# Attention in 32 units with 32x64 score products, ahead of a gated FFN

## The chip, the cores and the metric

The kernel runs on one core of a Trainium2 chip. The metric is the device time of one execution in microseconds (us). Engines carry the names of the profile: PE (TensorE matmul; PEld is its weight load), DVE (VectorE), ACT (ScalarE), POOL (GpSimd), SP (SyncE, which issues the loads). L12 is line 12 of the kernel.

## The reference

```python
def _attn_ref(q, k, v):                       # q, k, v: (8, 8, 576, 64)
    scores = scale * np.matmul(q, k.transpose(0, 1, 3, 2))
    rel = pos[:, None] - pos[None, :]
    mask_local = (rel >= 0) & (rel < stride)          # stride 32, heads 0 to 3
    mask_strided = (rel >= 0) & (pos[None, :] % stride == pos[:, None] % stride)
    scores = np.where(masks[None], scores, -1e9)      # then a softmax over keys
    return np.matmul(attn, v)

def _moe_ref(x, w_gate, w_val, w_out, rms_g):   # x: 4608 tokens of 8 heads x 64 = 512
    rms = np.sqrt(np.mean(x * x, axis=-1, keepdims=True) + 1e-06)
    xn = x / rms * rms_g
    g = xn @ w_gate                                   # 512 -> 1536
    silu = g * (1.0 / (1.0 + np.exp(-g)))
    return silu * (xn @ w_val) @ w_out                # 1536 -> 512
```

A query of heads 0 to 3 sees the 32 latest keys; a query of heads 4 to 7 sees the keys at distance 0, 32, 64, ..., so after a sort of the sequence by position modulo 32 (the "residue order") its at most 18 keys are neighbours.

## The kernel before

**FFN.** Tokens come in nine chunks of 512. For chunks 0 to 6 a chunk runs through 12 slots `u` of 128 hidden columns. In a slot, `slot_g` and `slot_v` issue 12 matmuls each into the banks `g` and `v` (L971), ACT and DVE form silu(g) x v in the tile `e` (L984, L986, L997), `slot_h` splits it into a float32r high and low part (`hh` L1004, `hl` L1013), and `slot_o` of the slot before issues 12 matmuls (L1028) into the four `acc` banks. All of these are 128x128 by 128x512 float32r matmuls, three for each product of split operands; weights and activations are split into high and low parts on the chip. Each 12 matmuls into a bank end in work on ACT and DVE before that bank is free again. Chunks 7 and 8 are taken together by `pair_of_chunks`, with seven products of sums of blocks in place of eight (L1357, L1522); their operands (`raw`, sums of `raw` halves, high and low parts) are built beforehand on DVE, ACT and POOL.

**Attention.** It makes the `raw` chunks that the FFN reads; tokens of chunk c+1 are made while chunk c runs. There are 96 work units: a batch row, a pair of heads `p` and a third `j` of the sequence, each of up to two tiles of 96 queries (heads 0 to 3) or of 126 and 108 (heads 4 to 7) for both heads. For a unit, `step_s` issues the scores on PE, adds the mask, finds the row maxima (DVE), exponentiates each tile (ACT, L694, with the sum), and normalizes (POOL, L703); `step_t` transposes the probabilities; `step_o` multiplies by the values (L783) for groups of up to four units and copies the result to `raw` (L818 ACT, L820 DVE). Scores have three forms: the first units add the mask on PE (L644) and multiply float32 queries by keys that lie in weight slots with the other head's rows at zero (L650); a few then use plain float32 products of 64 rows (L654) with the mask on DVE; from unit 27 on, q and k are split into high and low parts (`split`: ACT L541, DVE L546) and a tile is one float32r matmul of 128x256 (L639), whose two halves DVE adds with the mask (L675, L679, L681) ahead of the maximum (L682). Transposes are PE products against an identity (L757, copied out at L761) for the first 21 units and 32x32 stream transposes on DVE (L746) later.

**From chunk to chunk.** When the `raw` tile of a chunk is complete, squares are added up in `ssq`, a product with ones (L876, two matmuls; L857 for chunk 1, L838 for chunk 0) gives the sum over the 512 features in every partition, ACT takes the root (L912), DVE the reciprocal in four parts (L915) and scales `raw` (L919), and `convert` splits it into `xh` and `xl` (L932, L947), which the first `g` matmuls of the chunk read. `last_root` does the same for chunk 8 (L1110, L1114, L1117, L1119).

**Order.** Work is recorded with a cost, what it reads and writes, and a due time; the class `Plan`, a list scheduler, then fixes the order of instructions on every engine. `CO = 99` leaves PE's order free; `BA` and `BM` shift the due times of attention and of the FFN. The prologue does the first 15 units, with weights being loaded and split on DVE, ACT and POOL through chunk 0.

Of the kernel before, what the change touches and what calls it, by code (L numbers as in the profile page):

```python
# [34 lines left out]
RES = [7, 7, 6, 6, 6]  # L35
RES0 = [0, 7, 14, 20, 26]
NEG = -1.0e9
NCST = 510
# [16 lines left out]
BA = 30000.0  # L55
BM = 60000.0
# [60 lines left out]
CO = 99  # L117
# [32 lines left out]
class Plan:  # L150
# [7 lines left out]
    def __init__(self):  # L158
        self.ops = []
        self.writer = {}  # L160
        self.readers = {}
        self.lengths = []
        self.serial = False
        self.last_pe = None
        self.early = []
        self.lift = []
        self.boost = 0.0

    def op(self, eng, cost, at, fn, reads=(), writes=(), bytes_=0, rel=0.0, lock=(), tab=None, port=False, chain=False, also=None, early=0.0):
# [16 lines left out]
        deps.discard(i)  # L186
        if eng == "PE":
            if self.serial:
                deps.add(self.last_pe)
            self.last_pe = i  # L190
# [40 lines left out]
    def latest(self, users, took, length):  # L231
# [7 lines left out]
        for _ in range(n):  # L239
# [12 lines left out]
            for d in ops[i][1]:  # L252
                t = start[i] + (0.0 if on[d] == e and not ops[d][2] else self.lat(i)) + long[d] - ops[d][0][on[d]][0] + self.early[d]
                ready[d] = max(ready[d], t)
# [5 lines left out]
    def forward(self, users, due, hold, due2=None, hold2=None):  # L260
# [6 lines left out]
        def enter(i):  # L267
            ways, deps, _, rel, _, _, _ = ops[i]
            ready[i] = {e: max([end[d] + (0.0 if on[d] == e and not ops[d][2] else self.lat(i)) for d in deps] + [rel]) for e in ways}
# [74 lines left out]
def attn_moe(ctx: ExitStack, tc: tile.TileContext, qT: bass.AP, kT: bass.AP, vl: bass.AP, vs: bass.AP,  # L344
# [12 lines left out]
    ident = sbt([P, P], "ident")  # L357
    cb = sbt([P, 382], "cb", BF16)
    mloc = cb[:LQ, 0:256].rearrange("p (t k) -> p t k", k=P)
    m7 = cb[:126, 256:382]  # L360
    m6 = cb[:108, 256:364]
# [16 lines left out]
    def pair_of(i):  # L378
        k = (i % NPAIRS if i < 12 else i % 2) if i < n_pro else 0
        if k:  # L380
            return (acc01, acc23)[k - 1] if k == 2 else acc01, k, (f"a{2 * k - 2}", f"a{2 * k - 1}")
        return pair_, 0, ("b0", "b1")
    banks = {"g": bank["g"], "v": bank["v"], "b0": pair_[:, 0], "b1": pair_[:, 1], "a0": acc[0], "a1": acc[1], "a2": acc[2], "a3": acc[3]}
    mxs = [sbt([P, 2, 2], f"mx{i}") for i in range(2)]
    raw = [sbt([P, KC, CH], f"raw{i}") for i in range(NX)]
    low = sbt([P, QKN], "qk")
    stat = [mxs + [sbt([P, 2, 2], f"mx{i}") for i in range(2, 4)], [sbt([P, 2, 2, 2], f"su{i}") for i in range(4)]]
    SW = S + PAD
    xx = [sbt([P, SW], f"xx{i}") for i in range(2)] + [low[:, SW * i:SW * i + SW] for i in range(3)]
    vts = [sbt([P, 2, NLT, D], f"vt{i}") for i in range(2)]  # L390
    spare = [sbt([P, CH], f"x{n}{kc}") for n in "hl" for kc in range(KC)]
    pbuf = [sbt([P, CH], f"pp{i}") for i in range(NPB)]
    rcol = few[:, 12:16]
    tbufs = [sbt([P, CH], f"pT{i}") for i in range(NTB)]
    tbuf = tbufs[0]
# [44 lines left out]
    for x in range(5):  # L440
        op("Pool", 100, -1, lambda x=x: nc.gpsimd.memset(xx[x][:, 0:PAD], 0.0), writes=[("xp", x)])
    for x in range(NPB):
        op("Pool", 600, -1, lambda x=x: nc.gpsimd.memset(pbuf[x], 0.0), writes=[("pp", x)])

    for i in range(4):
        op("Pool", 70, -1, lambda i=i: nc.gpsimd.memset(stat[1][i][:, :, :, 1:2], 1e-9), writes=[("st", i)])
# [1403 lines left out]
```

## Time and profile before

| what | value |
|---|---|
| runs | 1012.08, 1014.07, 1016.27 us (median 1014.07) |
| profiled execution, its span | 1011.5 us |
| first and last 128x512 matmul of the FFN | starts at 32.70 us, ends at 1007.42 us |
| granted PE clock | 0.9 and 0.7 of full speed in the first two slices of 25 us, then 0.9 or more |
| attention on PE, records of matmuls | L783 704, L639 252, L650 88, L654 114, L757 78, L644 30 |

The page gives, for each engine, the time it was busy as a share of the span, the chain of work that ended last, and groups of instructions by line. A float32 matmul leaves two records, a float32r or bfloat16 matmul one. Matmuls are pipelined, so a matmul's duration on the page (about 0.39 us for a 128x512 one) is longer than the distance from its start to the next start; that distance is what a matmul costs.

### The profile page before, as it was taken

Reading aid. Unit: us, or ns where it says so; the run is one execution under the profiler, and the core shown is the slowest. Engines: PE = TensorE matmul, PEld = TensorE weight load, DVE = VectorE, ACT = ScalarE, POOL = GpSimd, SP = SyncE. Lnnn points to the kernel's source line nnn. Section 1 sums busy time; section 2 is a strip of 40 time slices with the busy share of each in tenths; the row PEclk is TensorE's granted clock in tenths of the full one; section 3 lists DMA queues with packets and bytes.
Section 4 is the critical chain, followed back from the end, with each engine's and each line's share of the span. In section 5 each row is a group of like instructions: output and inputs, shape, how many; then the busy total and the mean of one; then the engine's idle time right before and its main releaser. Section 6 shows DMA issues by size and latency. Waiting matters only on the chain.

```text
span 1011.5 us, 15391 instructions
## 1 busy us (share of the span) xinstructions
PE 991.0 (98%) x5104; PEld 805.3 (80%) x5104; DVE 844.7 (84%) x1745; ACT 572.0 (57%) x1502; POOL 417.3 (41%) x390
## 2 busy tenths in 40 slices
PE   8899998999999999999999999999999999999998
PEld 6678775888878888878878888887888878888886
DVE  5699999898888788679888878788988798988891
ACT  7899867554755555455555565555555444344440
POOL 6222457324662332533425432256643343565300
PEclk9799999999999999999999999999999999999999
DMA  9886342532432331532242422333332101120452
GB/s 314 271 286 227 129 137 98 177 109 91 161 133 92 102 124 61 178 99 93 92 132 94 141 97 105 99 116 118 114 114 79 42 1 42 39 87 1 156 167 73
DMA packets 52559, 121.11 MB, mean 120 GB/s; under 512 B 5312, under 2 KB 21248, under 8 KB 52480
## 3 DMA queue, kind: packets, MB, share of 16 engines
q1 hardware_dynamic: 51712, 119.28, 35.3%
q10 hardware_dynamic: 768, 0.85, 0.3%
q8 instruction: 40, 0.66, 0.3%
q14 instruction: 39, 0.32, 0.1%
HBM read 98.09 MB, written 22.02 MB: 119 GB/s over the span
## 4 chain that ended last, share of the span: by engine, by line
PE 80%; DVE 12%; ACT 3%; DMA 2%; issue 2%; ACTq 0%; DVEq 0%
PE g L971 18%; PE v L971 18%; PE acc L1028 18%; PE g L1357 3%; PE v L1357 3%; PE pair L1357 3%; PE pair L783 3%; PE pair L639 3%; DVE qk L546 2%; PE v L1522 2%; PE acc L1522 2%; PE acc L1357 2%; PE g L1522 2%; DVE raw L919 1%; DVE pT L746 1%
## 5 line engine op out<-in xcount | busy, mean ns | idle before, releaser
L971 PE MATMUL g<-xh,wg 128*128 128x512 f32 x672 | 211.8, 397 | 4.4 <-DVE e L986 3.4
L971 PE MATMUL v<-xh,wv 128*128 128x512 f32 x664 | 208.2, 395 | 1.8 <-DVE e L997 0.9
L1028 PE MATMUL acc<-or,hh 128*128 128x512 f32 x672 | 208.7, 392 | 0.0
L1013 POOL TENSOR_TENSOR hl<-e,hh 128x512 fp32r<-128x512 f32 x84 | 115.7, 1378 | 219.7 <-ACT hh L1004 200.0
L694 ACT ACTIVATE pp<-pp,mx 96x128 f32<-96x128 f32 (+2 forms) x296 | 114.0, 388 | 73.1 <-DVE mx L682 59.5
L703 POOL TENSOR_TENSOR pp<-pp,mx 96x512 f32<-96x512 f32 (+3 forms) x87 | 88.3, 1016 | 156.3 <-DVE mx L700 111.9
L971 PEld LDWEIGHTS g<-xh,wg 128*128 128x128 f32 x672 | 122.5, 189 | 31.1 <-DVE e L986 5.0
L1028 PEld LDWEIGHTS acc<-or,hh 128*128 128x128 f32 x672 | 124.5, 188 | 26.3 <-ACT ssq L1039 0.4
L971 PEld LDWEIGHTS v<-xh,wv 128*128 128x128 f32 x664 | 121.9, 189 | 28.6 <-DVE e L997 2.6
L971 PE MATMUL g<-xl,wg 128*128 128x512 f32 x336 | 132.1, 393 | 0.2 <-POOL xl L947 0.2
L1028 PE MATMUL acc<-or,hl 128*128 128x512 f32 x336 | 131.0, 390 | 0.0
L971 PE MATMUL v<-xl,wv 128*128 128x512 f32 x332 | 129.7, 391 | 0.0
L746 DVE STREAM_TRANSPOSE pT<-pp 32x128 f32<-32x128 f32 (+1 forms) x376 | 109.5, 291 | 12.0 <-POOL pp L703 7.0
L1004 ACT CAST hh<-e 128x512 fp32r<-128x512 f32 x84 | 52.3, 622 | 89.8 <-PE acc L1028 80.5
L984 ACT ACTIVATE e<-g 128x512 f32<-128x512 f32 x84 | 50.0, 596 | 80.0 <-PE g L971 71.5
L541 ACT CAST qk<-xx 64x576 fp32r<-64x576 f32 x138 | 88.7, 670 | 5.3 <-PE pair L639 3.8
L546 DVE TENSOR_TENSOR qk<-xx,qk 64x576 fp32r<-64x576 f32 x92 | 82.8, 900 | 6.6 <-ACT qk L541 4.1
L986 DVE SCALAR_TENSOR_TENSOR e<-e,g 128x512 f32<-128x512 f32 x84 | 57.4, 684 | 28.9 <-ACT e L984 28.2
L971 PEld LDWEIGHTS g<-xl,wg 128*128 128x128 f32 x336 | 63.5, 189 | 14.7 <-POOL xl L947 0.6
L1028 PEld LDWEIGHTS acc<-or,hl 128*128 128x128 f32 x336 | 63.1, 188 | 13.6
L971 PEld LDWEIGHTS v<-xl,wv 128*128 128x128 f32 x332 | 62.5, 188 | 13.5
L997 DVE SCALAR_TENSOR_TENSOR e<-e,v 128x512 f32<-128x512 f32 x83 | 56.9, 686 | 15.0 <-PE v L971 11.1
(515 smaller groups left out, 1799.8 us busy)
## 6 DMA issues: line engine op xcount, KB each, us to landing
or<-wos SPq DMA_DIRECT2D x72, 512.0 KB, 3.4
xx<-in_qT_dram SPq DMA_DIRECT2D x26, 288.0 KB, 2.8
xx<-in_kT_dram SPq DMA_DIRECT2D x25, 288.0 KB, 4.1
wg<-in_wgv_dram SPq DMA_DIRECT2D x12, 512.0 KB, 9.8
vt<-in_vl_dram SPq DMA_DIRECT2D x16, 384.0 KB, 3.4
wv<-in_wgv_dram SPq DMA_DIRECT2D x12, 512.0 KB, 7.0
or<-in_wo_dram SPq DMA_DIRECT2D x12, 512.0 KB, 4.2
wos<-or SPq DMA_DIRECT2D x12, 512.0 KB, 3.0
```

What stands on the lines that cost most here:

```text
L541: nc.scalar.copy(out=d, in_=s)
L546: (nc.gpsimd if eng == "Pool" else nc.vector).tensor_tensor(out=d, in0=s, in1=y.bitcast(F32), op=ALU.subtract)
L694: nc.scalar.activation(out=pv[:, h, x], in_=sp[h][:, x] if i < PM else pv[:, h, x], func=AF.Exp, scale=0.125 if i < PM else 1.0, bias=mx[: ...
L703: (nc.vector if e == "DVE" else nc.gpsimd).tensor_tensor(out=pv, in0=pv, in1=mx.unsqueeze(3).broadcast_to([m, 2, nt, n]), op=ALU.mult)
L746: nc.vector.transpose(out=dst[32 * y:32 * y + 32, :, 32 * x:32 * x + 32], in_=src[32 * x:32 * x + 32, :, 32 * y:32 * y + 32])
L971: nc.tensor.matmul(out=out, lhsT=wt[:, w, sl], rhs=xhl[x, kc], start=(kc == 0 and i == 0), stop=(kc == KC - 1 and i == 2))
L986: op("DVE", dve(CH), at + MO, lambda: nc.vector.scalar_tensor_tensor(out=e, in0=e, scalar=1.0, in1=bank["g"], op0=ALU.add, op1=ALU.mult), ...
L997: op("DVE", dve(CH), at + MO, lambda: nc.vector.scalar_tensor_tensor(out=e, in0=e, scalar=0.5, in1=bank_of(c, ("v", u))[0], op0=ALU.mult, ...
L1013: (nc.vector if n == "DVE" or h else nc.gpsimd).tensor_tensor(out=hl[h], in0=e, in1=hh[h].bitcast(F32), op=ALU.subtract)
L1028: nc.tensor.matmul(out=acc[t], lhsT=x[h][:, sl], rhs=wt[:, w], start=(u == 0 and i == 0), stop=(u == NU - 1 and i == 2))
L1357: nc.tensor.matmul(out=banks[bk], lhsT=w, rhs=X[a, k].tile(y), start=start and k == 0 and i == 0, stop=stop and k == 1 and i == 2, skip_gr ...
L1522: nc.tensor.matmul(out=banks[bks[j]], lhsT=tile(v, k, j), rhs=x.tile(y), start=start and k == 0 and i == 0, stop=stop and k == KT - 1 and ...
```

## The change

Attention is cut into 32 units, a batch row and head pair each (`unit_s`, `unit_o`), four in the prologue and four in each chunk 0 to 6. All heads use one geometry: queries in blocks of 32, each with 64 keys (its own 32 and the 32 before); strided heads come in residue order. Scores are 36 plain float32 products of 32 queries by 64 keys (K = 64). The softmax runs on one tile of 96x768: 3 blocks of 32 queries on the partitions; 2 heads, 6 tiles and 64 keys along the row. For units 0 to 3 PE adds the mask and ACT exponentiates twelve parts. For the others DVE scales and adds the mask, takes the maximum and subtracts it (this step on DVE or POOL), ACT exponentiates the whole tile, and DVE sums and normalizes (this too on DVE or POOL). Six stream transposes lead to twelve value products of 64x96. The split of q and k, the zero-padded keys in weight slots and the transposes on PE are gone. The input `vs` is dropped; `vl` holds the values of all heads.

The order changes too: `CO = 1` makes PE follow the order as written from chunk 1 on, until the last slot of chunk 6; scores come at slots 0, 2, 5, 7 of a chunk (`SAT`), value products at slots 2, 4, 7, 9 (`OAT`), all in the bank pair `pair`, where the chunk sums of squares go as well (`b0` instead of `g`). Operands of the Strassen-like part that lay in `qk` move to `pT0`, `pT1`, `xx2` and `xx3`.

```diff
-CO = 99
+CO = 1
+SAT = (0, 2, 5, 7)
+OAT = (2, 4, 7, 9)
-BA = 30000.0
-BM = 60000.0
+BA = 0.0
+BM = 0.0
...
+    units = [(b, p) for b in range(NB) for p in ((2, 3, 0, 1) if b == NB - 1 else range(NH // 2))]
+    n_pro = 4
...
+        def scores():
+            if onpe:
+                for h in range(2):
+                    nc.tensor.matmul(out=sp[:, h], lhsT=identb[:LQ, :LQ], rhs=mk, start=True, stop=False, skip_group_check=True)
+            for t in range(NLT):
+                for x in range(3):
+                    for h in range(2):
+                        r = (TOP, BOT)[h]
+                        q0 = LQ * t + 32 * x
+                        nc.tensor.matmul(out=pr[32 * x:32 * x + 32, h, KW * t:KW * t + KW], lhsT=tq[r, q0:q0 + 32], rhs=tk_[r, q0:q0 + KW],
+                                         start=not onpe, stop=True, skip_group_check=True)
...
+            op("DVE", dve(2 * MW), 0, biased, reads=["cb"] + keys_, writes=[pk])
+            op("DVE", dve(2 * MW), 0, lambda: nc.vector.tensor_reduce(out=mx, in_=pv, axis=AX.X, op=ALU.max, negate=True), reads=[pk], writes=[sk])
+            op("Pool", pool(2 * MW), 0, lambda e: both(e).tensor_tensor(out=pv, in0=pv, in1=mx.unsqueeze(2).broadcast_to([LQ, 12, KW]), op=ALU.add),
+               reads=[sk], writes=[pk], also=[("DVE", dve(2 * MW), True)])
+            op("ACT", act(2 * MW), 0, lambda: nc.scalar.activation(out=buf[:LQ], in_=buf[:LQ], func=AF.Exp), writes=[pk], tab="exp")
+            op("DVE", dve(2 * MW), 0, lambda: nc.vector.tensor_reduce(out=su, in_=pv, axis=AX.X, op=ALU.add), reads=[pk], writes=[sk])
...
+        for x in range(3):
+            def swap(x=x):
+                for y in (x, x + 1):
+                    nc.vector.transpose(out=dst[32 * y:32 * y + 32, :, 32 * x:32 * x + 32],
+                                        in_=pv[32 * x:32 * x + 32, :, 32 * (y - x):32 * (y - x) + 32])
...
+        def values():
+            for t in range(NLT):
+                for h in range(2):
+                    y = (NLT * h + t) * LQ
+                    nc.tensor.matmul(out=pr[64 * h:64 * h + 64, t // 3, LQ * (t % 3):LQ * (t % 3) + LQ], lhsT=vt[:, h, t, :], rhs=pT[:, y:y + LQ],
+                                     start=True, stop=True, skip_group_check=True)
...
+            plan.serial = c >= CO
+            for k in range(4):
+                i = 4 * (c + 1) + k
+                if u == SAT[k]:
+                    load(i)
+                    load_v(i)
+                    unit_s(i)
             plan.boost = BM if c >= CB else 0.0
             slot_g(c, u)
...
+            for k in range(4):
+                i = 4 * (c + 1) + k
+                if u == OAT[k]:
+                    unit_o(i)
...
-                    rms(c + 1, "g", at + RMS)
+                    rms(c + 1, "b0" if c else "g", at + RMS)
```

How PE's instructions move at the end of a chunk: these rows of PE start at the sum of squares for chunk 2, before the change. `g`, `v`, `acc` are the FFN's banks, `pair` that of attention, `x36` a repeated row.

```order
L876 MATMUL g<-srt,onesr 128x512
L876 MATMUL g<-pT_2630,onesr 128x512
L971 MATMUL v<-xh_452,wv_1645 128x512 x2
...
L1028 MATMUL acc_70<-or_2314,hh_105 128x512 x2
L1028 MATMUL acc_70<-or_2314,hl_749 128x512
L971 MATMUL g<-xh_452,wg_1603 128x512 x2
...
L639 MATMUL pair<-qk 96x256 x4
```

The same place of the changed kernel, from the sum to the first `g` product of the next chunk.

```order
L664 MATMUL pair<-srt,onesr 128x512
L664 MATMUL pair<-pT_2388,onesr 128x512
L754 MATMUL g<-xh_433,wg_1534 128x512 x2
...
L754 MATMUL v<-xh_433,wv_1572 128x512 x2
...
L811 MATMUL acc_69<-or_2197,hh_91 128x512 x2
...
L519 MATMUL pair<-xx_78,xx_77 32x64 x36
L754 MATMUL g<-xh_433,wg_503 128x512 x2
```

Before, `g`, `v` and `acc` products of the last slot alternate bank by bank behind the sum, with score products among them; now they stand as all `g`, all `v`, all `acc`, and the next chunk's first scores lie right ahead of its first `g` product. Ahead of the Strassen-like part, PE before the change (the sum of chunk 7, the root of chunk 8 comes later among these rows):

```order
L876 MATMUL pair<-srt,onesr 128x512
L876 MATMUL pair<-pT_7081,onesr 128x512
L1028 MATMUL acc_70<-or_6708,hh_105 128x512 x2
...
L971 MATMUL g<-xh_452,wg_1254 128x512 x2
...
L1028 MATMUL acc_71<-or_7038,hl_749 128x512
L1357 MATMUL g<-raw_7191,wg_444 128x512 x6
```

The same place after it:

```order
L664 MATMUL pair<-srt,onesr 128x512
L664 MATMUL pair<-pT_6621,onesr 128x512
L893 MATMUL pair<-pp,onesr 128x512 x2
L754 MATMUL g<-xh_433,wg_1534 128x512 x2
...
L811 MATMUL acc_70<-or_6435,hl_713 128x512
L1143 MATMUL g<-raw_6719,wg_503 128x512 x6
L1143 MATMUL v<-raw_6719,wg_610 128x512 x6
```

Before, 153 products of the FFN lie between L876 and the first L1357; now both sums stand together and 36 lie between them and the first L1143. On DVE a unit of attention now reads as follows (one unit from its first pass to its transposes, with the FFN's L769 and L780 between):

```order
L525 SCALAR_TENSOR_TENSOR pp<-pair,cb 96x768
L543 TENSOR_REDUCE st_76<-pp 96x12
L544 TENSOR_TENSOR pp<-pp,st_76 96x768
L769 SCALAR_TENSOR_TENSOR e<-e,g 128x512
L547 TENSOR_REDUCE st_76<-pp 96x12
L550 TENSOR_SCALAR st_76<-st_76 96x12
L551 RECIPROCAL st_76<-st_76 96x12
L553 TENSOR_TENSOR pp<-pp,st_76 96x768
L780 SCALAR_TENSOR_TENSOR e<-e,v 128x512
L559 STREAM_TRANSPOSE pT_85<-pp 32x12x32 x6
```

Where a work unit had its hi and lo parts, mask passes and two groups of transposes, three times for a head pair, one sequence of 13 instructions now stands.

More of the change, by code (lines that the diff above doesn't have):

```diff
@@ L268, in enter @@
             ways, deps, _, rel, _, _, _ = ops[i]
-            ready[i] = {e: max([end[d] + (0.0 if on[d] == e and not ops[d][2] else self.lat(i)) for d in deps] + [rel]) for e in ways}
+            ready[i] = {e: max([end[d] - (self.TAIL["PE"] if self.after[i] == d else 0.0) + (0.0 if on[d] == e and not ops[d][2] else self.lat(i))
+                                for d in deps] + [rel]) for e in ways}
             for e in ways:
@@ new lines, in load @@
+    def load(i):
+        b, p = units[i]
+        for x, (src, t) in enumerate(((qT, xq[i % 2]), (kT, xk[i % 2]))):
+            off = 0 if x == 0 else PAD
+            parts = [(0, 3 * LQ), (3 * LQ, S)] if i == 0 else [(0, S)]
+            for z, (a, e) in enumerate(parts):
+                op("SP", 430, 0, lambda t=t, src=src, off=off, a=a, e=e: nc.sync.dma_start(out=t[:, off + a:off + e], in_=src[b, p, :, a:e]),
+                   writes=[("xx", 2 * (i % 2) + x) if z or len(parts) == 1 else ("xa", x)], bytes_=P * (e - a) * 4)
+        if i == 0:
+            op("SP", 430, 0, lambda: nc.sync.dma_start(out=identb, in_=consts[:, 2 * MW:2 * MW + P]), writes=[("hl", 0)], bytes_=P * P * 2)
+            op("SP", 430, 0, lambda: nc.sync.dma_start(out=cb, in_=consts[:, 0:2 * MW]), writes=["cb"], bytes_=P * MW * 4)
+            op("ACT", 300, 0, lambda: nc.scalar.copy(out=ident, in_=identb), reads=[("hl", 0)], writes=["ident"])
@@ new lines, in load_v, with banks_of @@
+    def load_v(i):
+        b, p = units[i]
+        op("SP", 430, 0, lambda: nc.sync.dma_start(out=vts[i % 2], in_=vl[b, p].rearrange("r (h t d) -> r h t d", h=2, t=NLT)),
+           writes=[("vt", i % 2)], bytes_=P * 3000)
+        if i == 0:
+            op("SP", 430, 0, lambda: nc.sync.dma_start(out=gt, in_=gain), writes=["gt"], bytes_=2048)
+    def banks_of(i):
+        k = i % 3 if i < n_pro else 0
+        pr = (pair_, acc01, acc23)[k]
+        return pr, [("S", k)] + (["b0", "b1"], ["a0", "a1"], ["a2", "a3"])[k] * (i < n_pro and k > 0)
@@ L820, in evac @@
                         nc.vector.tensor_copy(out=d, in_=s)
-            op("ACT", act(nt * m, True) + 60 * (len(moves) - 1), at_of(i) + 1500, evac, reads=[("T", pn)], lock=locks[x % 2:x % 2 + 1],
-               writes=[("raw", c % NX, p) for c in cs] + ["free2"] * (i == 11), also=way("e", ("DVE", dve(nt * m) + 80 * (len(moves) - 1), False)), early=EARLY if b == NB - 1 else 0.0)
+            op("ACT", act(3 * LQ, True) + 60 * (len(moves) - 1), 0, evac, reads=keys_,
+               writes=[("raw", c % NX, p) for c in cs], also=way("e", ("DVE", dve(3 * LQ) + 80 * (len(moves) - 1), False)))
+        if b < NB:
+            square(b, p, 0)
     def square(c, p, at):
```

567 lines of the change are left out of this document (127 added, 440 removed), and 2 rows, old and new, of the table xplace.

## The prediction

> **What bounds the kernel now.** I read the page first, then the timeline of PE, then windows that count the matmuls of one line in each stage.
>
> ```profile
> span 1011.5 us, 15391 instructions
> PE 991.0 (98%) x5104; PEld 805.3 (80%) x5104; DVE 844.7 (84%) x1745; ACT 572.0 (57%) x1502; POOL 417.3 (41%) x390
> PE 80%; DVE 12%; ACT 3%; DMA 2%; issue 2%; ACTq 0%; DVEq 0%
> ```
>
> TensorE is busy for 98% of the span and holds 80% of the chain that ended last. So the time is what PE must issue, plus the few stretches in which it waits. In the timeline of PE (start, duration, line, count) I look for the price of one 128x512 product of the two GEMMs, and for the frame around them:
>
> ```profile
> 32.70 1.22 PE L971 MATMUL g<-xh,wg 128*128 128x512 f32 x2
> ...
> 233.28 0.63 PE L1028 MATMUL acc<-or,hh 128*128 128x512 f32 x2
> ...
> 233.97 0.63 PE L1028 MATMUL acc<-or,hh 128*128 128x512 f32 x2
> ...
> 234.67 0.62 PE L1028 MATMUL acc<-or,hh 128*128 128x512 f32 x2
> ...
> 1006.58 0.84 PE L1522 MATMUL v<-wv,xl 128*128 128x512 f32 x3
> ```
>
> Six products start in 234.67 - 233.28 = 1.39 us, so one costs 0.23 us; over long quiet stretches it comes to 0.2268. The program has 2016 on L971, 1008 on L1028, 504 on L1357 and 252 on L1522: 3780, or 857.3 us. The first starts at 32.70 and the last ends at 1007.42, with 4.1 us behind it. So 974.7 - 857.3 = 117.4 us between first and last is small matmuls and waits. The next rows (windows of L971, then of L1028) say in which stage they lie; the count is in brackets.
>
> ```profile
> 32.60:200.00 167.40, 99.87 (x369) 0.97 0.54 185
> 300.00:800.00 500.00, 324.34 (x1302) 1.00 0.32 106
> ...
> 32.60:200.00 167.40, 44.40 (x168) 0.97 0.54 185
> 300.00:800.00 500.00, 169.65 (x656) 1.00 0.32 106
> ```
>
> From 32.6 to 200 us there are 537 products, 121.8 us of 167.4: **45.6 us** go elsewhere. From 300 to 800 us there are 1958, 444.1 of 500: 55.9 us, or 11 per 100. So the first stage after the prologue loses 27 per 100 us, over twice the later rate. Two of its waits, in brackets behind the rows:
>
> ```profile
> 154.70 1.12 PE L857 MATMUL g<-ssq,ones 128*128 128x512 f32 x2 [1.08 <-POOL ssq L852]
> ...
> 168.67 0.96 PE L971 MATMUL g<-xh,wg 128*128 128x512 f32 x2 [2.59 <-DVE e L986]
> ```
>
> **The price of attention on PE, before.** Timeline rows of the three forms:
>
> ```profile
> 146.54 0.68 PE L654 MATMUL pair<-qk,xx 64*96 64x128 f32 x8
> 147.15 0.50 PE L971 MATMUL v<-xh,wv 128*128 128x512 f32 x1
> ...
> 230.53 0.39 PE L1028 MATMUL acc<-or,hl 128*128 128x512 f32 x1
> 230.85 1.31 PE L783 MATMUL pair<-pT,vt 128*64 128x96 f32 x24
> 231.99 0.54 PE L783 MATMUL pair<-srt,vt 108*64 108x108 f32 x8
> 232.47 0.50 PE L971 MATMUL v<-xh,wv 128*128 128x512 f32 x1
> ...
> 277.03 0.39 PE L971 MATMUL v<-xl,wv 128*128 128x512 f32 x1
> 277.26 0.64 PE L639 MATMUL pair<-qk 128*96 128x256 f32 x4
> 277.74 0.39 PE L971 MATMUL g<-xh,wg 128*128 128x512 f32 x1
> ```
>
> L639: from 277.03 to 277.74 is 0.71 us, less the 0.23 of the product ahead: 0.48 for one work unit. L783: from 230.53 to 232.47 is 1.94, less 0.23: 1.71 us for four work units. A head pair of a batch row has three, so it costs 3 x 0.476 + 1.71 x 3/4 = **2.71 us**.
>
> **After, the value products.** Twelve plain float32 products of 64x96, the shape of L783. A float32 product leaves two records; two tiles run at once, the next pair 82.5 ns later (the 24 records above, sixteen of them 96 wide, take 1.14 us). 12 x 82.5 ns + 0.24 for switching in and out = **1.23 us**.
>
> **After, the score products (the unknown).** 36 products of 32x64, 72 records, on six places of the array: two row halves (heads) by three column strips. The trace has rows of two halves (L654, eight records of width 128 in 0.61 us, so pairs 109 ns apart) and of two columns (L783), none of both. At width 64 a record would last half of 109, 56 ns. If only the heads overlap, 18 x 2 x 56 ns + 0.24 = **2.25 us**; if all six do, a third, **0.9 us**. In L783 two columns overlap fully, weight loads included; in L654 two rows do; so I stand nearer to the lower end, but 72 starts at some 7 ns each (the gap in a pair of records) and a second record that waits for its first take away part of it. I take 62 ns for the two records of a head pair on a strip, 18 of them: **1.35 us**, and keep both ends.
>
> [...]
>
> A unit then costs 1.35 + 1.23 = 2.58 us of PE, only 0.13 less than now: on the 23 head pairs that L639 serves, 3 us. **The change is worth something only where the first units now pay more.**
>
> **The first 200 us.** Transposes leave PE, masks too except for four units, and the first products need no zero-padded keys. I followed the new order by hand, with durations from these rows:
>
> ```profile
> L679 DVE SCALAR_TENSOR_TENSOR pp<-pair,cb 96x512 f32<-96x512 f32 x22 | 15.0, 682 | 1.7 <-PE pair L639 1.3
> L746 DVE STREAM_TRANSPOSE pT<-pp 32x128 f32<-32x128 f32 x320 | 96.4, 301 | 10.5 <-POOL pp L703 6.2
> L675 DVE SCALAR_TENSOR_TENSOR pp<-pair,cb 96x256 f32<-96x256 f32 x22 | 8.2, 412 | 0.8 <-PE pair L639 0.4
> L546 DVE TENSOR_TENSOR qk<-xx,qk 64x576 fp32r<-64x576 f32 x92 | 82.8, 900 | 6.6 <-ACT qk L541 4.1
> L694 ACT ACTIVATE pp<-pp,mx 96x128 f32<-96x128 f32 x156 | 60.8, 393 | 41.2 <-DVE mx L682 36.4 <-DVE mx L699 3.8 <-DVE mx L687 0.8
> ...
> xx<-in_qT_dram SPq DMA_DIRECT2D x26, 288.0 KB, 2.8
> xx<-in_kT_dram SPq DMA_DIRECT2D x25, 288.0 KB, 4.1
> ```
>
> 256 more elements cost 270 ns, so 768 cost 0.95 us; a transpose of 384 wide about 0.57. A unit on DVE: five passes (scale and mask, maximum, add, sum, normalize) 4.75, six transposes 3.4, small ones 0.3: 8.4 us, 32 of them 270. Now L546 (82.8), the transposes, the mask passes and maxima take about 400 by their groups. DVE falls by some 130 us to near 710; the normalization leaves POOL and the hi and lo copies leave ACT, whose exponentials fall from four of 0.39 in a work unit to one of 768 in a unit, some 0.8 by the same slope. All this is behind PE and I cost it at nothing: from one unit's scores to its value products two slots of 36 big products lie (16 us), and its chain is 8.4 + 0.8 and the passes of the FFN between. The loads of a unit go to the buffers that the unit before last left, at least two slots earlier; they land after 3 to 4 us by the last two rows, so I cost them at nothing too. The prologue, estimated: loads and the first scores and maximum until 9 us (the first exponential now can't be much earlier), three units of twelve exponentials at 0.38 from start to start, 13.8, two copies between, 1.8, then normalize 1, transposes 3.4, value products 1.2, copy and hi part 1.2, steps 2: 33.5 us to the first product instead of 32.7. The fourth unit ends some 7 us later, and its squares, their sum and the root allow the spread matrix near 49; of the time until then 21 products, a score and a value burst use 7.4, so about 7.6 is waited, and with 1.0 for sums and spread **8.6 us** stand between the first products. In chunk 0 DVE stays full with weight conversion, but has about half the attention work beside it: 4 us of waits, where the timeline now has gaps of some 9.
>
> **What loses cover.** The order of PE is fixed as written from chunk 1 on. At a chunk boundary 36 products lie between the sum of squares and the first product of the next chunk (8.2 us, and one score burst); before, it was 36 and then 45 to 48. The chain behind that sum now:
>
> ```profile
> 272.68 0.40 PE L876 MATMUL g<-srt,onesr 128*128 128x512 f32 x1
> 283.02 0.70 PE L971 MATMUL g<-xh,wg 128*128 128x512 f32 x2 [1.04 <-ACT xh L932]
> ...
> 274.69 0.69 ACT L912 ACTIVATE srt<-g,few 128x512 f32<-128x512 f32 x1
> 276.35 2.56 DVE L915 RECIPROCAL srt<-srt 128x128 f32<-128x128 f32 x3
> 280.73 1.55 DVE L919 SCALAR_TENSOR_TENSOR raw<-raw,few,srt 128x512 f32<-128x512 f32 x2
> ```
>
> Root 0.7, four reciprocals 3.4, scaling 0.7, hi 0.6, lo 0.7 to 1.4, steps between: 8 to 9 us against 9.5 of cover when nothing else stands on DVE. A FFN pass in between (0.7) or the next chunks' lo parts break it: 0 to 2.5 us at each of five boundaries, I take 1.2, **6 us**. In front of the Strassen part it is worse:
>
> ```profile
> 796.14 0.40 PE L876 MATMUL pair<-srt,onesr 128*128 128x512 f32 x1
> ...
> 833.00 1.20 PE L1357 MATMUL g<-raw,wg 128*128 128x512 f32 x4 [0.16 <-DVE e L986]
> ...
> 826.13 3.48 DVE L1311 TENSOR_TENSOR raw<-raw,raw 128x512 f32<-128x512 f32 x2
> ```
>
> Now 36.9 us lie between the sum and the first product that needs its result; after, 36 products, 8.2 us. Operands built on DVE from both roots (eight reciprocals 7.4, eight scalings 6 to 9, sums as in L1311, lo parts) reach the pair bank's products at 18 to 21 us, where PE stands at 15: 0 to 9 us lost, I take **5.5**.
>
> **The sum.** 33.5 to the first product + 857.3 + 28 score bursts x 1.35 = 37.8 + 29 value bursts x 1.23 = 35.7 + 8.6 left of the prologue + 5.3 for the sums of the chunks (as now) + waits 4 + 6 + 5.5 + 2 = 17.5 + 4.1 behind = 999.8, against 1011.5. The median of the runs is 2.6 above that execution; I add this: **1002 us**.
>
> **The rivals.**
> - *All six tiles overlap:* 28 x 0.45 less, **990**. For it: full overlap of two tiles in both directions.
> - *The strips take turns (slower):* one mechanism, the burst of L519. At 2.25 us the 28 cost 25 us more: **1027**. The deciding point, where gain and loss cancel, is 1.35 + 12 / 28 = 1.8 us. A limit on starts would do the same: 1.8 us is 22 ns for each of 72 records, and the rows above have none denser than 1.14 us / 24 = 47 ns over a whole burst. [...] The two records of a pair, 7 ns apart in the trace of L654 and L783, speak against a floor across tiles.
> - *Cover lost is at its upper end:* 5 x 2.5, 9 at the end, 7 in chunk 0 instead of 15.5 together: 13 more, **1015**.
> - *Nothing measurable:* the 45.6 us come from weight conversion on DVE and stay, because 0.13 us per unit is all: then 10 to 13 of the gain go, **1014**. The transposes and masks of that stage, which do vanish, speak against it.
>
> **How the numbers follow.** Forecast (995 to 1008) 0.40, six tiles 0.20, strips in turn 0.17, cover lost 0.15, nothing 0.08. A measurement of this kernel tells 0.5% from no change: 1009.0 to 1019.1 is same. Faster: 0.40 + 0.20 + the lower part of cover lost 0.04 = 0.64; slower: 0.17 + 0.03 of cover lost = 0.20; same 0.16. The range reaches from 985 (0.9 us bursts and few waits) to 1027 (2.25 us).
>
> **What would show it.** The burst of 72 records of L519 between two big products (1.35, 0.9 or 2.25 us), that of L572 (1.23), the first L754 near 33.5, PE's idle time before the first L754 behind each L664 (1.2) and between L893 and the first products of L1143 (5.5), DVE near 710 us. A burst above 1.8 us, or boundary waits over 3 us each, would make the forecast wrong.

## The result and the profile after

The changed kernel took 1031.26 us (median of four runs, 1029.86 to 1034.42), the kernel before 1014.12: a ratio of 1.0175, 95% interval 1.0151 to 1.0200, some 17 us slower. The forecast was 1002 us. Two executions of run e10 below took 2465 and 3383 us, far from all others, and its figures are those of the other five. The page of the profiled execution, the rows that answer to those of before (the two with digits are tenths of a slice of 26 us, PE busy and clock granted):

```profile
span 1032.7 us, 17181 instructions
PE 979.9 (95%) x6920; PEld 784.8 (76%) x6920; DVE 709.9 (69%) x1078; ACT 376.6 (36%) x748; POOL 287.0 (28%) x232
PE   4799779899999999999999999999999988999998
PEclk6699989999999999999999999999999999999999
PE 75%; DVE 17%; ACT 3%; issue 2%; DMA 2%; SPq 0%; POOL 0%; ACTq 0%; DVEq 0%; POOLq 0%
```

Every engine does less: PE 11 us, DVE 135, ACT 195, POOL 130. Yet the span is 21 us longer (the profiled execution of the changed kernel was the longest of its four). The first row of digits says where to look: PE has holes in its first eight slices (to 206 us) and in slices 33 and 34 (826 to 878 us), and its clock is low at the start. Windows of the changed kernel, of the `g` and `v` products (L754), then of the `acc` products (L811); the count is in brackets:

```profile
41.40:200.00 158.60, 89.86 (x336) 0.94 0.52 177
300.00:800.00 500.00, 317.40 (x1316) 1.00 0.34 112
...
41.40:200.00 158.60, 41.83 (x148) 0.94 0.52 177
300.00:800.00 500.00, 159.59 (x660) 1.00 0.34 112
```

A big product is 0.2268 us, so counts of products done turn into time. This makes a ledger of the two profiled executions:

| at | before | after | after is behind by |
|---|---|---|---|
| the first big product | 32.7 us | 41.5 us | 8.8 us |
| 200 us | 537 products | 484 | 12.0 us |
| 300 us | 918 | 869 | 11.1 us |
| 800 us | 2874 | 2843 | 7.0 us |
| the end of the last one | 1007.4 us | 1028.8 us | 21.3 us |

So 8.8 us are lost in the prologue, some 3 more in the stage to 200 us, 14 at the end, and 4 are won in the quiet middle (1976 products against 1958 in 500 us), where attention is what the prediction calls it: small bursts between big products. Two of them in the timeline of the changed kernel:

```profile
316.62 0.39 PE L754 MATMUL g<-xl,wg 128*128 128x512 f32 x1
316.94 1.21 PE L572 MATMUL pair<-pT,vt 128*64 128x96 f32 x24
318.08 0.74 PE L754 MATMUL v<-xh,wv 128*128 128x512 f32 x2
...
341.19 0.39 PE L811 MATMUL acc<-or,hl 128*128 128x512 f32 x1
341.51 0.97 PE L519 MATMUL pair<-xx,xx 64*32 64x64 f32 x72
342.41 0.74 PE L754 MATMUL g<-xh,wg 128*128 128x512 f32 x2
```

From start to start, less the 0.23 of the product ahead, a value burst costs 1.23 us and a score burst 0.99. In the prologue the same bursts cost more, and PE waits for keys and for the softmax of one unit after the other:

```profile
9.48 1.52 PE L519 MATMUL acc<-xx,xx 64*32 64x64 f32 x72 [1.47 <-DMA xx<-in_kT_dram]
16.46 1.52 PE L519 MATMUL acc<-xx,xx 64*32 64x64 f32 x72 [4.67 <-DMA xx<-in_kT_dram]
21.81 2.19 PE L572 MATMUL pair<-pT,vt 128*64 128x96 f32 x24 [3.82 <-DVE st L550]
41.47 1.20 PE L754 MATMUL g<-xh,wg 128*128 128x512 f32 x2
...
0.00:41.50 41.50, 22.41 (x397) 16.70 (x397) 27.40 (x58) 23.46 (x114) 5.81 (x13) 0.65 0.88 303
```

The last row is a window: the granted clock is 0.65 over these 41.5 us, where it was 0.92 over the same stretch before. At the end, the timeline of PE, one row of DVE and two of ACT:

```profile
833.36 0.39 PE L664 MATMUL pair<-pT,onesr 128*128 128x512 f32 x1
835.77 0.73 PE L893 MATMUL pair<-pp,onesr 128*128 128x512 f32 x2 [2.02 <-ACT srt L695]
...
850.53 0.39 PE L811 MATMUL acc<-or,hl 128*128 128x512 f32 x1
855.03 2.25 PE L1143 MATMUL acc<-pT,wg 128*128 128x512 f32 x6 [4.11 <-ACT srt L822]
857.08 0.63 PE L1143 MATMUL pair<-xx,th 128*128 128x512 f32 x1
857.50 0.63 PE L1143 MATMUL pair<-xx,tl 128*128 128x512 f32 x1
...
848.41 4.82 DVE L902 SCALAR_TENSOR_TENSOR raw<-raw,few,xx 128x512 f32<-128x512 f32 x4
852.61 0.62 ACT L1046 CAST or<-raw 128x512 fp32r<-128x512 f32 x1 [2.48 <-DVE raw L902]
854.40 0.58 ACT L822 COPY srt<-acc 128x512 f32<-128x512 f32 x1
```

PE stands 2.0 us before L893 and 4.1 us before the third group of L1143. The second wait is for the bank `acc`: it ends with L822, a copy of chunk 6's result out of `acc`, and ACT came to these copies only behind L1046, which had waited 2.5 us for DVE to scale `raw` by the second root (L902). Behind the longer wait the products start 0.43 us apart (857.08, 857.50) instead of 0.23. In the changed kernel 44 big products start 0.38 to 0.45 us behind the one ahead, 8.7 us more than they should take; before there were 11, 2.1 us.

### The profile page after: what moved, and what is told of

Its sections match the earlier page's. It is cut to its first block, busy times and chain, and to the rows that moved or that the text cites. A ratio compares the mean times of both kernels' runs of the same rounds, so it can differ in the third digit from the quotient of the medians.

```text
span 1032.7 us, 17181 instructions
## 1 busy us (share of the span) xinstructions
PE 979.9 (95%) x6920; PEld 784.8 (76%) x6920; DVE 709.9 (69%) x1078; ACT 376.6 (36%) x748; POOL 287.0 (28%) x232
## 4 chain that ended last, share of the span: by engine, by line
PE 75%; DVE 17%; ACT 3%; issue 2%; DMA 2%; SPq 0%; POOL 0%; ACTq 0%; DVEq 0%; POOLq 0%
PE acc L811 18%; PE v L754 18%; PE g L754 17%; PE pair L572 3%; PE pair L1143 3%; PE g L1143 3%; PE v L1143 3%; DVE srt L698 2%; PE pair L519 2%; PE g L1308 2%; PE v L1308 2%; DVE raw L702 2%; PE acc L1308 2%; PE acc L1143 2%; DVE pT L559 1%
## 5 line engine op out<-in xcount | busy, mean ns | idle before, releaser
L754 PE MATMUL g<-xh,wg 128*128 128x512 f32 x672 | 215.2, 402 | 6.9 <-DVE e L769 4.3
L811 PE MATMUL acc<-or,hh 128*128 128x512 f32 x672 | 211.8, 396 | 6.4 <-DVE or L1447 3.1
L754 PE MATMUL v<-xh,wv 128*128 128x512 f32 x664 | 210.3, 397 | 2.6 <-POOL wv L1447 1.5
L811 PEld LDWEIGHTS acc<-or,hh 128*128 128x128 f32 x672 | 127.4, 191 | 37.2 <-DVE or L1447 4.2
L754 PEld LDWEIGHTS g<-xh,wg 128*128 128x128 f32 x672 | 125.9, 191 | 36.7 <-ACT or L1430 3.1
L754 PEld LDWEIGHTS v<-xh,wv 128*128 128x128 f32 x664 | 122.0, 188 | 33.1 <-DVE e L780 3.0
L769 DVE SCALAR_TENSOR_TENSOR e<-e,g 128x512 f32<-128x512 f32 x84 | 57.5, 684 | 113.6 <-ACT e L767 113.0
L754 PE MATMUL g<-xl,wg 128*128 128x512 f32 x336 | 132.9, 396 | 0.0
L811 PE MATMUL acc<-or,hl 128*128 128x512 f32 x336 | 132.2, 393 | 0.0
L754 PE MATMUL v<-xl,wv 128*128 128x512 f32 x332 | 129.4, 390 | 0.0
L559 DVE STREAM_TRANSPOSE pT<-pp 32x384 f32<-32x384 f32 x192 | 109.1, 568 | 3.1
L780 DVE SCALAR_TENSOR_TENSOR e<-e,v 128x512 f32<-128x512 f32 x83 | 56.8, 684 | 64.8 <-PE v L754 64.1
L754 PEld LDWEIGHTS g<-xl,wg 128*128 128x128 f32 x336 | 64.2, 191 | 15.1 <-DVE xl L730 1.1
L811 PEld LDWEIGHTS acc<-or,hl 128*128 128x128 f32 x336 | 63.8, 190 | 13.5
L754 PEld LDWEIGHTS v<-xl,wv 128*128 128x128 f32 x332 | 62.3, 188 | 13.7
L525 DVE SCALAR_TENSOR_TENSOR pp<-pair,cb 96x768 f32<-96x768 f32 x28 | 26.6, 951 | 50.6 <-PE pair L519 50.6
L640 POOL TENSOR_TENSOR ssq<-ssq,srt 128x512 f32<-128x512 f32 x21 | 31.1, 1481 | 73.9 <-ACT srt L635 73.9
L572 PEld LDWEIGHTS pair<-pT,vt 128*64 128x64 f32 x720 | 32.9, 144 | 17.2 <-issue 12.9
L572 PE MATMUL pair<-pT,vt 128*64 128x96 f32 x720 | 38.7, 260 | 6.4 <-DVE st L550 3.8
```

The source lines that it names most:

```text
L559: nc.vector.transpose(out=dst[32 * y:32 * y + 32, :, 32 * x:32 * x + 32], in_=pv[32 * x:32 * x + 32, :, 32 * (y - x):32 * (y - x) + 32])
L572: nc.tensor.matmul(out=pr[64 * h:64 * h + 64, t // 3, LQ * (t % 3):LQ * (t % 3) + LQ], lhsT=vt[:, h, t, :], rhs=pT[:, y:y + LQ], start=Tru ...
L640: op("Pool", pool(CH), at, lambda e: (nc.vector if e == "DVE" else nc.gpsimd).tensor_tensor(out=ssq, in0=ssq, in1=roots["srt"], op=ALU.add ...
L754: nc.tensor.matmul(out=out, lhsT=wt[:, w, sl], rhs=xhl[x, kc], start=(kc == 0 and i == 0), stop=(kc == KC - 1 and i == 2))
L769: op("DVE", dve(CH), at + MO, lambda: nc.vector.scalar_tensor_tensor(out=e, in0=e, scalar=1.0, in1=bank["g"], op0=ALU.add, op1=ALU.mult), ...
L780: op("DVE", dve(CH), at + MO, lambda: nc.vector.scalar_tensor_tensor(out=e, in0=e, scalar=0.5, in1=bank_of(c, ("v", u))[0], op0=ALU.mult, ...
```

## The experiments

Theory A: three places lose time, the prologue, the stage in which weights are converted, and the end, and none of it is the price of the bursts. Rival B: the fixed order of PE costs by itself. Within the middle stage, theory D: DVE's total work binds; rival K: the length of a unit's chain does. Single executions of the same instructions differ: e1, which issues the same instructions on PE and DVE as the changed kernel in the first stage, had 886 products done at 300 us, the changed kernel 869 and, repeated in e15, 873. So one execution of that stage tells nothing below 4 us.

**e1, an earlier end.**

```diff
+SAL = (0, 2, 3, 5)
+OAL = (2, 4, 5, 7)
...
-                if u == SAT[k]:
+                if u == (SAT if more else SAL)[k]:
...
-                if u == OAT[k]:
+                if u == (OAT if more else OAL)[k]:
...
-            if u == NU - 2:
-                if more:
-                    rms(c + 1, "b0" if c else "g", at + RMS)
-                else:
-                    rms(c + 1, "b0", at + RMS)
-                    last_root()
+            if u == NU - 2 and more:
+                rms(c + 1, "b0" if c else "g", at + RMS)
+            if u == NU - 4 and not more:
+                rms(c + 1, "b0", at + RMS)
+            if u == NU - 3 and not more:
+                last_root()
```

> In chunk 6 alone the scores come at slots 0, 2, 3, 5 and the value products at 2, 4, 5, 7, the sum of chunk 7 at slot 8 and that of chunk 8 at slot 9, with PE's order still fixed; the rest is the changed kernel. Theory A (the end is slow because only 36 big products lie between the sums and the Strassen-like part): the stalls behind 826 us (3.2 with both sums, 0.6, 4.3 and the slow clock behind it, 1.8) shrink from about 11 us to 2 to 4, and the span falls from 1032.7 by 7 to 10, to 1022 to 1026. Rival B (the fixed order of PE itself costs, wherever the sums stand): less than 3 us. Rival C (DVE has too much work for that stage): the stall only moves to a later product, gain under 4 us.

Measured 1024.29 us (one run) against 1031.26. The sums and the first Strassen-like product in its timeline, without a wait ahead of any:

```profile
816.28 0.40 PE L666 MATMUL pair<-pT,onesr 128*128 128x512 f32 x1
824.70 0.63 PE L895 MATMUL pair<-pp,onesr 128*128 128x512 f32 x2
841.51 1.55 PE L1145 MATMUL g<-raw,wg 128*128 128x512 f32 x6
```

Now 25 us lie between the first sum and L1145. What lies behind 800 us besides big products falls from 15.9 to 5.0 us. Two value bursts of 1.2 us are in the 15.9 and one in the 5.0, so the end itself gains 9.7 us. The whole gains only 7.0: between 300 and 800 us this execution did 1956 products against 1976, with a wait of 2.1 us at 637 us (the copies out of `acc`, L824, waited for their tiles to be stored) that the trace of the changed kernel does not have. Theory A holds for the end: the cover was missing. B and C, as stated, fall, since PE's order was still fixed and DVE had the same work.

**e2, the kernel before with PE's order fixed.**

```diff
-CO = 99
+CO = 1
```

> The kernel before, with PE's order fixed as written from chunk 1 on until the last slot of chunk 6, as the change has it, and nothing else of the change. Rival B (the fixed order costs): 10 us or more above the kernel before, spread over the chunks. Theory A (it is cover at particular places): within 3 us of the kernel before in chunks 2 to 5, and a loss only where the order as written leaves little between a sum and its use.

Measured 1115.76 us (one run), 102 above the kernel before. For this kernel rival B's forecast came true, and theory A's was far off. The two waits of PE that are largest in total, for L546 (10 times, 25.2 us) and for L912 (5 times, 7.7 us):

```profile
529.90 0.63 PE L639 MATMUL pair<-qk 128*96 128x256 f32 x4
532.18 1.22 PE L971 MATMUL g<-xh,wg 128*128 128x512 f32 x2 [1.65 <-ACT srt L912]
...
547.47 0.50 PE L639 MATMUL pair<-qk 128*96 128x256 f32 x1 [5.29 <-DVE qk L546]
549.77 0.93 PE L639 MATMUL pair<-qk 128*96 128x256 f32 x3 [1.80 <-DVE qk L546]
```

The sum stands in bank `g`, so `g` waits for the root that reads it; and the scores, written ahead of the `g` products, wait for the split of q and k. A fixed order is as good as the order that was written: what stood first for no reason now holds up all behind it. The changed kernel has the sum in `pair` and no split of q and k; its middle shows neither wait. The two make 33 of the 102 us; the rest is not taken apart here.

**e3, loads of the third unit ahead of the first weights** (release times of the weight loads + 4.5 us).

```diff
-        fetch(key, WL0 + WLP * x)
+        fetch(key, WL0 + WLP * x + 4500.0)
```

> The changed kernel with all weight loads of the first ring released 4.5 us later, so that SP issues the q and k of the third unit ahead of the first weights. Theory A1 (the late keys of the third unit, landed at 16.4 us, hold up the prologue): they land near 12, and the first big product moves from 41.5 to 36 to 38.5 us. Rival A2 (the softmax of one unit after the other on DVE and ACT, and the two probability buffers, decide): the first big product stays within 1 us of 41.5.

1030.11 us (one run); the third unit's scores start at 12.9 instead of 16.5 us, but the first big product only moves to 40.5, where three executions with the loads as they were had it at 41.5, 41.1 (e1) and 40.8 (e15). Most of what the load had held up then waited for the softmax: rival A2.

**e4, PE kept busy in the prologue.** Behind each unit's scores and behind its sums, a dummy product:

```diff
+    def keep(n, keys_):
+        for _ in range(n):
+            op("PE", 860, 0, lambda: nc.tensor.matmul(out=bank["g"], lhsT=ones, rhs=ebuf, start=True, stop=True),
+               reads=["ones", "wz"] + keys_, writes=["g"])
...
         unit_s(i)
+        keep(1, banks_of(i)[1][:1])
+        keep(1, [("st", i % 2)])
```

> The changed kernel with eight 128x512 float32 dummy products into the idle bank g, one behind the scores and one behind the softmax sums of each unit of the prologue, so that PE is idle for less of the first 40 us. Theory A3 (waits in the prologue lower the granted clock, 0.65 over the first 41.5 us, and this lengthens the bursts that stand in the chain): the clock of this stretch rises to 0.8 or more, a value burst falls from 2.1 to about 1.25 us, the first nine big products take 2.1 instead of 4.1 us, and the first 200 us gain 2 to 4 us. Rival: the clock rises but the dummy products stand in the way of the bursts as long as they save, gain within 1 us; or the clock does not follow the load of PE at all.

1027.63 us (one run). The window of the prologue:

```profile
0.00:41.50 41.50, 32.08 (x420) 18.65 (x421) 29.45 (x62) 27.08 (x119) 6.29 (x13) 0.87 0.92 329
```

The clock rises from 0.65 to 0.87, the first big product comes at 37.9 us instead of 40.8 to 41.5, and 499 products are done at 200 us instead of 484 to 492. DVE, ACT and POOL have the same instructions in the same order up to 300 us, so the dummy products alone made this. Idle PE costs twice here, once as a wait and once in what follows it: the first value burst takes 1.21 us instead of 2.19. The first nine big products still came at the slow rate, 0.43 us apart.

**e5, no maximum in units 4 to 11.**

```diff
+NMX = range(4, 12)
...
+            if i not in NMX:
               op("DVE", ..., tensor_reduce(out=mx, ..., op=ALU.max, negate=True), ...)
               op("Pool", ..., tensor_tensor(out=pv, in0=pv, in1=mx..., op=ALU.add), ...)
```

> The changed kernel, with the maximum and its subtraction left out for units 4 to 11 (the exponential of the masked scores as they are), which takes two passes of 0.95 us, 1.9 us, off DVE in each of these units, some 15 us up to 220 us. Theory D (from 100 to 200 us DVE is full, and each us less on DVE is one less of waiting on PE): big products between 100 and 200 us rise from 285 by 25 to 50, and 200 us is left with 6 to 12 us more done. Rival E (the waits there come from the order, each behind one late operation, whatever DVE's load): fewer than 15 more.

1025.04 us (one run); 915 products at 300 us, 29 more than in e1, 6.6 us, for about 15 us of DVE. In the windows from 100 to 200 us, the changed kernel and then e5 (PE, PEld, DVE, ACT, POOL busy):

```profile
100.00:200.00 100.00, 83.24 (x601) 63.38 (x600) 95.89 (x144) 43.41 (x78) 33.33 (x24) 0.93 0.39 131
```

```profile
100.00:200.00 100.00, 91.19 (x740) 69.85 (x739) 90.89 (x140) 48.75 (x88) 34.67 (x26) 0.98 0.44 150
```

PE has 8 us more to do, with DVE the only engine near full. That fits D and K alike, since the chain is 1.9 us shorter too.

**e6, normalization of units 4 to 11 on POOL.**

```diff
+PNU = range(4, 12)
...
-        op("Pool", pool(2 * MW), 0, lambda e: both(e).tensor_tensor(out=pv, in0=pv, in1=su.unsqueeze(2).broadcast_to([LQ, 12, KW]), op=ALU.mult),
-           reads=[sk], writes=[pk], also=[("DVE", dve(2 * MW), True)])
+        def norm(e):
+            both(e).tensor_tensor(out=pv, in0=pv, in1=su.unsqueeze(2).broadcast_to([LQ, 12, KW]), op=ALU.mult)
+        if i in PNU:
+            op("Pool", pool(2 * MW), 0, lambda: norm("Pool"), reads=[sk], writes=[pk])
+        else:
+            op("Pool", pool(2 * MW), 0, norm, reads=[sk], writes=[pk], also=[("DVE", dve(2 * MW), True)])
```

> The changed kernel, with the normalization of units 4 to 11 on POOL, as the kernel before had it, instead of DVE: 0.95 us of DVE for 1.5 to 1.8 us of POOL, eight times. Theory D: 7 to 8 us less DVE work, 12 to 30 more big products between 100 and 200 us than 285. Rival F (POOL lengthens what DVE does beside it, and the chain of a unit grows by 0.8 us): no more products than in the changed kernel, and longer means of the two-input operations on DVE.

1030.06 us (one run), 887 products at 300 us, as in e1: no gain. The window from 100 to 200 us:

```profile
100.00:200.00 100.00, 88.56 (x661) 67.39 (x662) 88.25 (x137) 43.92 (x79) 32.60 (x23) 0.93 0.41 139
```

DVE has 7.6 us less to do there than in the changed kernel, and 304 products are done in it against 285, as theory D said; but 11 fewer were done before it, and at 200 us it has 492, as many as e1. Two passes of the weights went from POOL back to DVE, and from 56 to 300 us PE waited 3.3 us for weight parts of POOL and 4.4 us for those of ACT, where e1 had 1.5 and 0.4. So less work on DVE is not enough by itself. F's sign did not come: the two-input weight passes on DVE took 0.75 and 0.73 us in the mean, not more than the 0.87 and 0.84 in the changed kernel. What took the gain away is not shown.

**e7, the mask of the first units on DVE.**

```diff
-MPE = (0, 1, 2, 3)
+MPE = ()
```

> The changed kernel, with the first four units done like all others: mask, maximum, subtraction and sum on DVE, one exponential of 768 on ACT instead of twelve of 64. DVE gets 2.9 us more per unit in the first 35 us, where it now idles for 14 us; ACT gets 14 us back and can scale weights earlier. Theory G (in the prologue ACT's exponentials bound the weight conversion and the units): the first big product comes 2 to 6 us earlier than 41.5 and 200 us sees 10 to 25 more products done. Rival H (DVE is then the bound of the prologue): the first product comes at 41 to 46.

1029.36 us (one run), first product at 42.8 us: rival H. DVE is busy for 26.7 of the first 35 us instead of 21.0, and what ACT gained was not needed.

**e8, the edits of e1, e3 and e4 in one kernel.**

> The earlier end of e1, the dummy products of e4 and the later weight loads of e3 in one kernel. If the three parts of theory A add up: e1 and e4 gained 10 and about 4 us, e3 about 1; 1031 - 15 = 1014 to 1018 us, no more than 0.4% above the kernel before, with the stage from 100 to 200 us still at 285 to 300 big products.

1017.47 us in nine runs, a ratio to before of 1.0057 (1.0036 to 1.0079): 13.8 us less than the changed kernel, where e1, e3 and e4 gained 7.0, 1.2 and 3.6 by one run each. The parts roughly add up, and some 5 us remain.

**e9 and e10, e8 without the maximum in units 4 to 31, and in 4 to 11** (e5's edit on top of e8).

```diff
+NMX = range(4, 32)     # e9
+NMX = range(4, 12)     # e10
```

> e8 with the maximum and its subtraction left out in all units from 4 on. Theory D: up to 200 us this gives the 5 to 7 us that e5 gave; from 300 us on, where PE waits for nothing, the 1.9 us less on DVE per unit bring nothing. Against e8 5 to 8 us less: 1009 to 1012 us, at or just below the kernel before. Rival: DVE also holds PE up later, then 12 us or more.

> e8 with the maximum and its subtraction left out in units 4 to 11 only. Theory D: the same time as e9 within 2 us, since DVE binds only while weights are converted. Rival: e9 is faster than this by 4 us or more.

1010.19 us in ten runs (ratio 0.9963, 0.9947 to 0.9978) and 1008.26 us in five (0.9950, 0.9932 to 0.9969). The two agree within 2 us; off the first stage, 38 us less of DVE bring nothing. These are below both kernels, by 4 to 6 us from the kernel before, but only without a pass that a softmax for any input needs.

**e11, the kernel before with six work units' transposes on DVE.**

```diff
-TP = 21
+TP = 15
```

> The kernel before, with the transposes of work units 15 to 20 moved from PE to DVE (TP = 15 for 21), which takes some 3 us of small matmuls off PE and puts about 11 us on DVE between 50 and 160 us. Theory D (DVE is the bound there, PE's small matmuls are not): slower by 2 to 6 us, with 10 to 25 big products fewer done at 200 us than the 537 of the kernel before. Rival (what leaves PE is gained, as the prediction had it): 1 to 3 us faster.

1023.25 us, a ratio of 1.0089 (1.0064 to 1.0114): 9 us slower, more than expected. Windows to 200 us of the transposes (L746), of L971 and of L1028:

```profile
0.00:200.00 200.00, 22.09 (x77) 0.97 0.59 203
...
0.00:200.00 200.00, 94.62 (x345) 0.97 0.59 203
...
0.00:200.00 200.00, 44.11 (x156) 0.97 0.59 203
```

Nine us more of transposes on DVE (13.1 before), and 501 products instead of 537: 8 us. Of these, 2.5 us lie ahead of the first big product (35.2 instead of 32.7), where the order changed too but the moved transposes do not stand; some 6 us are left for the nine. What left PE was no gain.

**e12, the changed kernel with a free order on PE.**

```diff
-CO = 1
+CO = 99
```

> The changed kernel with PE's order left to the scheduler in all chunks (CO = 99). Theory A: from 300 to 800 us the fixed order costs and gains nothing, 1974 big products within 10; at the end the sums come only some ten products earlier, so the end stays 10 us or more behind the kernel before. Rival B (the fixed order costs): 20 products more from 300 to 800 us, or the loss at the end gone.

1024.78 us in one run, some 6 less than the changed kernel. From 300 to 800 us it did 1985 products, nine more than 1976; behind 800 us 13.0 us remain besides big products instead of 15.9. At 200 us it has 492 products, as e1. So by this one run the fixed order costs a few us at most, and is neither the loss at the end nor that of the first stage. The change also sets `BA` and `BM` to 0; they act from chunk 2 on (`CB = 2`), so not in the first stage, and no run tests them.

**e13, e14, e15: DVE's work or the length of the chain?** e13 does one weight pass twice for 16 tiles, e14 puts three value bursts of chunks 0 and 1 a slot later, e15 is the changed kernel.

```diff
-        op("DVE", CD * dve(512), at, value, reads=[wk], writes=[zk], port=PORT)
+        for _ in range(1 + (x is not None and 8 <= x < 24)):
+            op("DVE", CD * dve(512), at, value, reads=[wk], writes=[zk], port=PORT)
```

```diff
+OAF = (3, 5, 8, 9)
...
-                if u == OAT[k]:
+                if u == (OAT if c > 1 else OAF)[k]:
```

> The changed kernel, with one DVE pass of the weight conversion done twice (the same result) for 16 of the weight tiles: about 16 x 0.66 = 10.6 us more of DVE before 200 us, none of it in the chain of an attention unit. Theory D (DVE's total work binds): 6 to 11 us slower than e15, with 25 to 50 big products fewer at 300 us. Rival K (the length of a unit's chain from scores to value products binds): within 3 us of e15.

> The changed kernel, with the value products of the first three units of chunks 0 and 1 one slot later (8 us more for the chain, the same work on every engine). Rival K: waits for transposes go, 4 to 8 us faster than e15. Theory D: within 3 us of e15, the waits only move to weight parts and FFN passes.

> The changed kernel, unchanged, as the measure for e13 and e14: 1028 to 1034 us by both theories.

e13 1042.77 us, e14 1027.34, e15 1031.23 (four runs each). DVE work outside the attention chain costs most of its length: 11.5 us, of which 9 are there when the 864th product is reached, that is two chunks' worth, for 16 passes that were to take 10.6 (15.3 by the trace). That is theory D. The extra slot for the chain gives 3.9 us, above the 3 that D allows and just below what K forecast, so rival K has a part too. How the loss divides between the two is not shown.

## Why the prediction was wrong

| term | forecast, us | measured, us |
|---|---|---|
| to the first big product | 33.5 | 41.5 |
| 28 score bursts | 37.8 | 27.8 |
| 29 value bursts | 35.7 | 35.7 |
| rest of the prologue, to the spread matrix | 8.6 | 7.3 |
| sums of the chunks | 5.3 | 4.5 |
| waits and slow products | 17.5 | 54.7 |
| behind the last product | 4.1 | 3.9 |

The last but one is what is left of 1032.7 us with 857.3 for the big products. The step that failed, and the largest part of that row, is "**In chunk 0 DVE stays full with weight conversion, but has about half the attention work beside it: 4 us of waits**". From the first big product to 200 us (chunk 0 ends near 185), the kernel before and then the changed one (PE, PEld, DVE, ACT, POOL busy):

```profile
32.70:200.00 167.30, 160.78 (x881) 125.32 (x880) 152.91 (x302) 133.21 (x345) 67.01 (x56) 0.97 0.54 185
```

```profile
41.50:200.00 158.50, 137.84 (x983) 106.32 (x984) 149.84 (x236) 96.59 (x170) 42.31 (x30) 0.94 0.52 176
```

PE idles for 20.7 us there instead of 4, where it idled for 6.5 before, and DVE does not get lighter: it is busy for 95% of the stretch, before for 91%. Up to the same point of the FFN, its 537th product, DVE has 15 us more to do (172.0 us before, 187.2 after):

```profile
0.00:199.80 199.80, 187.16 (x1094) 145.69 (x1095) 172.03 (x366) 157.47 (x448) 86.68 (x96) 0.97 0.61 206
```

```profile
0.00:216.10 216.10, 176.35 (x1527) 135.60 (x1528) 187.21 (x308) 123.79 (x291) 50.50 (x44) 0.88 0.58 196
```

I had compared DVE's attention work over the whole kernel (400 against 270 us; the page's 709.9 us for DVE is what I forecast) and put the ratio into a stage in which the kernel before had spared DVE. Windows to 200 us of before, transposes on DVE (L746) and normalization on POOL (L703):

```profile
0.00:200.00 200.00, 13.10 (x45) 0.97 0.61 207
...
0.00:200.00 200.00, 30.96 (x28) 0.97 0.61 207
```

And of after, transposes (L559) and normalization (L553), both on DVE:

```profile
0.00:200.00 200.00, 30.66 (x54) 0.88 0.60 203
...
0.00:200.00 200.00, 8.69 (x8) 0.88 0.60 203
```

The early units before had their masks and transposes on PE and their normalization on POOL. That made PE's bursts long, and I counted that as a cost to be saved; it was the price of keeping DVE free for weights. e11 shows it in the kernel before, e5, e10 and e13 in the changed one. The chain of a unit from its scores to its value products, which I had cost at nothing, has a part in this loss: 3.9 us by e14. The rival "Nothing measurable" named the weight conversion as the cause, but let the loss stay where it was; it grew. The one rival that came near the time, strips in turn at 1027 us, did so by luck: its burst of 2.25 us took 0.99.

The prologue: I took the chain of units as DVE's and ACT's alone, from durations at full speed. The slow clock (0.65 over the first 41.5 us) made 3 to 3.6 us of the miss of 8 (e4) and the third unit's loads one at most (e3). The rest I read from the trace but did not test: the third unit's exponentials wait 5.2 us for one of two probability buffers, and the fourth unit's scores for the copies out of their bank.

The end: the mechanism "cover lost" was right, and its size, 5.5 us and 9 at most, was too small. The loss was some 10 by e1: 4.1 us for the bank `acc`, which I had not seen (its copies stand on ACT behind the operands of the second root), 0.5 for an operand, 2.0 for L893, which stands in the fixed order behind a root it shares the bank pair with and which I had not seen either, 1.6 of slow clock (eight products 0.2 us late; the granted clock is 0.61 from 855 to 859 us), and 1.8 later on. The boundary waits (6 us forecast) did not come: from 300 to 800 us PE idles for 0.8 us in all, and at 404 us a score burst and the first `g` product follow without a wait.

The score burst was mis-sized the other way: 0.99 us instead of 1.35, close to the rival of six tiles at once. Its 72 weight loads, 106 ns each in the trace, lie within it beside the products (PEld busy for 0.81 us, PE for 0.97), so they cost nothing visible here. And 72 records in 0.75 us besides the 0.24 for switching, 10 ns each, do not bear out the limit on starts, 22 ns each, that the rival of strips in turn names as another cause.

## What to carry to other kernels

Compare an engine's work stage by stage, with what the old kernel had moved off it there; a total that falls by 135 us can hide a stage in which it rises, and there it can cost most of its own length. When an order becomes fixed, go through each instruction that then stands ahead of others and ask what it waits for. Cover between a sum and its use should be counted against the longest chain that hangs on it, copies that free a bank included, not the first one.

## What the hardware showed that I had not expected

A wait of PE can cost more than its length. In the changed kernel six waits behind the first big product are of 2.0 us or more (2.0 to 4.1); after five of them 3 to 12 big products started about 0.43 us apart instead of 0.23, so that the wait of 4.1 us took 1.6 more. None of the shorter waits, up to 1.6 us, was followed by this. The wait does not decide alone: ahead of L893 it is 2.02 us both in the changed kernel and in its repetition e15, and what follows differs. The row of L893 in e15, then the four us behind that wait in e15 and in the changed kernel (the granted clock is the third number from the end):

```profile
833.52 1.05 PE L893 MATMUL pair<-pp,onesr 128*128 128x512 f32 x2 [2.02 <-ACT srt L695]
...
833.50:837.50 4.00, 3.98 (x11) 3.13 (x11) 3.96 (x5) 0.76 (x2) 3.92 (x4) 0.57 0.00 0
```

```profile
836.00:840.00 4.00, 4.00 (x19) 3.28 (x19) 3.96 (x6) 1.44 (x3) 3.92 (x4) 1.00 0.00 0
```

The same holds in a prologue where PE idled for nearly half the time (busy for 22.4 of 41.5 us, granted clock 0.65): seven of the first nine products started as slowly. Waits of 2.0 us (e15) to 2.7 us between stretches of work were already followed by the slow rate; what decides beside their length is not shown. Six positions of the array (two row halves, three column strips) took 36 float32 products of 32x64 in 0.99 us, where two positions alone would have needed 2.25 by the prediction's estimate.
